# GpSimd's shifted bit pattern as 32-bit additions in five pieces, in a fused attention and gated-MLP kernel

## The chip, the cores and the metric

The kernel runs on one core of a Trainium2 chip. The metric is the device time of one execution in microseconds (us). In this document PE is the matmul engine, PEld its weight loads, ACT the activation engine, DVE the vector engine, POOL (GpSimd) the general-purpose engine, SP the queue that issues transfers. In this kernel PSUM is the memory that the matmuls write to and SBUF the working memory; an eviction copies a result out of PSUM into SBUF. The granted clock is the share of PE's full clock that the profile records as let through.

A time with no other remark is a median of runs. A ratio is the mean time of one kernel's fast runs over that of the other kernel's fast runs of the same rounds, so it isn't quite the ratio of the medians quoted beside it.

## The reference

Layer norm, then attention with 32 heads of size 16 over 2048 positions, plus a gated MLP, plus the input:

```
def reference(A_x, A_wqkv, A_wo, B_x, B_W_gate, B_W_up, B_W_down):
    x = A_x                       # 1 x 2048 x 512, bf16
    xn = _layernorm(x)
    # attention: softmax(q k^T * 16**-0.5) v, 32 heads, then @ wo
    # MLP: h = relu(xn @ W_gate) * (xn @ W_up);  h @ W_down
    return x + _A_ref(xn, A_wqkv, A_wo) + _B_ref(xn, B_W_gate, B_W_up, B_W_down)
```

Some 134 million exponentials are what makes it long: in the kernel before, the 647 instructions of ACT's part of them are busy 742.3 us of a span of 793.6.

## The kernel before

ACT computes most exponentials (647 instructions). For 108 groups of score tiles, DVE computes them instead (16 of these groups with help from GpSimd), by building bf16 bit patterns from an integer. One such group goes like this (cuts marked with `...`):

```
# d1: four evictions out of PSUM, 128x512 each: score -> integer bit pattern tp
e.tensor_scalar(dring[...].bitcast(U16), ps_b[...], 0.25 * LOG2E * 128.0, ..., op0=ALU.mult, op1=ALU.add)
# d2, d3, d5: correction terms from tp, on DVE, SBUF to SBUF
G.op("DVE", 600, ... bitwise_or ...,  lock=True, name="d2")
G.op("DVE", 600, ... bitwise_and ..., lock=True, name="d3")
G.op("DVE", 1140, ... tensor_tensor mult ..., lock=True, name="d5")
# the shifted pattern ts_ = tp + 36: on GpSimd in some groups, on DVE (d4) in the others
if g in on_pool:
    cuts = [2048 * k // N_ADD for k in range(N_ADD + 1)]          # N_ADD = 7
    for a, z in zip(cuts, cuts[1:]):
        o = G.op("POOL", 100 + int(P_NS * (z - a)),                # P_NS = 1.4
                 lambda e, a=a, z=z: e.tensor_scalar(b(ts_, U16)[:, a:z], b(tp, U16)[:, a:z], float(SHIFT), None, op0=ALU.add),
                 reads=[tp], ..., name="pm", lock=True)
else:
    G.op("DVE", 600, ... the same addition on all 2048 ..., name="d4", lock=True)
```

Four quadruples of matmuls per group (PV) then multiply the four patterns with the values; the last reads `ts_`.

Nothing here is dispatched at run time. `G.op(engine, duration, function, ...)` only records an instruction with an **assumed duration**. A planner then places all of them, and each engine gets a fixed list with semaphore waits. For the instructions with `lock=True` the planner keeps GpSimd and DVE apart: a piece on GpSimd is placed beside a DVE instruction without the mark, such as the eviction d1, and only if it is planned to end by about the end of that instruction:

```
if y.lock or at + o.dur > y.start + y.dur + self.SLIP:    # y: DVE's current instruction, SLIP = 100 ns
    continue
```

The softmax here doesn't subtract the row's maximum and nothing guards it: scores larger than these inputs give would overflow.

Of the kernel before, what the change touches and what calls it, by code (L numbers as in the profile page):

```python
# [9 lines left out]
U16 = mybir.dt.uint16  # L10
FP16 = mybir.dt.float16
ACTF = mybir.ActivationFunctionType
ALU = mybir.AluOpType
# [19 lines left out]
NWS = 3  # L33
NQ = 3
NDR = 9
N_ADD = 7
P_NS = 1.4
P_PRIO = -2.4
POOL_AT = ((), (2,), (), (6,), (), (1,), (), (2,), (), (3,), (), (2,), (), (2,), (), (4,), (), (1,), (), (3,), (), (4,), (), (2,), (), (3,), (), (1,), (), (1,), (), (1,))
KD = (1, 5, 9, 13)  # L40
# [36 lines left out]
SHIFT = 36  # L77
# [379 lines left out]
def bass_parallel_sum__mha_block__glu_gated_reglu__prompt_kernel(  # L457
# [16 lines left out]
    with ExitStack() as es:  # L474
        def sb(name, shape, dt):
            return es.enter_context(nc.sbuf_tensor(name, shape, dt))
# [3 lines left out]
        hmask = sb("hmask", [128, 2], FP32)  # L480
        expo = sb("expo", [128, 4], FP32)
        minus = sb("minus", [128, 1], FP32)
        warm = sb("warm", [128, 2], FP32)
        stats = sb("stats", [128, NT, 6], FP32)
        mv = sb("mv", [128, NT, 2], FP32)
# [34 lines left out]
        G = Graph()  # L520
# [23 lines left out]
             reads=[t_pid], writes=[t_pid], prio=-890)  # L544
        G.op("DVE", 100, lambda e: e.tensor_scalar(hmask[:, 1:2], pid[:, 0:1], 1.0 / 16.0, None, op0=ALU.mult),
             reads=[t_pid], writes=[t_mask], prio=-889)
        G.op("DVE", 100, lambda e: e.tensor_scalar(hmask[:, 0:1], pid[:, 0:1], -1.0 / 16.0, 1.0, op0=ALU.mult, op1=ALU.add),
             reads=[t_pid], writes=[t_mask0], prio=-888)
# [2 lines left out]
        G.op("POOL", 300, lambda e: e.affine_select(out=ident[:], in_=ident[:], compare_op=ALU.not_equal, fill=1.0,  # L551
                                                    base=0, pattern=[[-1, 128]], channel_multiplier=1),
             reads=[t_id], writes=[t_id], prio=-898)
        t_vones, t_woz, t_minus = Tile(), Tile(), Tile()
        G.op("POOL", 200, lambda e: e.memset(minus[:], -1.0), writes=[t_minus], prio=10)
        t_qz = [Tile(), Tile()]
        t_qt0 = Tile("qr", P_qr, [0])
        G.op("POOL", 500, lambda e: e.memset(qT[:, 0, :], 0.0), writes=[t_qt0], prio=-600)
# [4 lines left out]
             reads=[t_id32], writes=[t_id32], prio=60)  # L563
# [13 lines left out]
        for i in range(2):  # L577
            dma(lambda e, i=i: e.dma_start(q_scr[i, :, DH:2 * DH, :], qT[:, 0, :]), 128,
                reads=[t_qt0], writes=[t_qz[i]], prio=-600)
# [35 lines left out]
        for j in range(4):  # L615
            for ee in range(2):
                dma(lambda e, j=j, ee=ee: e.dma_start(Wo_p[32 * j:32 * j + DH, ee, :], wo_src[NGG - 1, j, ee, :, :]), 16,
                    reads=[t_woz], writes=[Tile()], prio=40)
# [579 lines left out]
        def score(e, bank, t):  # L1198
            c4, gg, ee, kt, j = t
            return e.matmul(bank, kT[32 * j:32 * j + 32, gg, 128 * kt:128 * kt + 128],  # L1200
                            qm[32 * j:32 * j + 32, t_q[(c4, gg)].slot, ee, :], start=True, stop=True, tile_position=(32 * j, 0))
# [3 lines left out]
        def dve_exp(g, u):  # L1205

            tp, tm, tn, ts_ = (Tile("dr", P_dr) for _ in range(4))
            t4 = [g + (j,) for j in range(4)]
            prev_d, mine = list(last_d), []
            for j, t in enumerate(t4):  # L1210
                ts = Tile("ds", P_b, D_BANKS)
                G.op("PE", 225, lambda e, t=t, ts=ts: score(e, ps_b[:, ts.slot, :], t), mode="row", rows=(j,), reads=[t_q[t[:2]], t_k[(t[1], t[3] // 4)], t_kfirst] + ([t_q1] if t[:3] == (0, 0, 1) else []), writes=[ts],
                     prio=u + D_WAIT, name="dsc", after=u - D_AHEAD, order=prev_d if D_SEQ else ())
                G.ops[-1].acq.append(tp)
                mine.append(G.ops[-1])
                o = G.op("DVE", 610, lambda e, j=j, ts=ts: e.tensor_scalar(dring[:, tp.slot, 512 * j:512 * j + 512].bitcast(U16), ps_b[:, ts.slot, :],  # L1216
                                                                    0.25 * LOG2E * 128.0, 128.0 * (127.0 - LOG2_SUM), op0=ALU.mult, op1=ALU.add),
                         reads=[ts], writes=[tp], prio=u - 960, name="d1")
                for w in tp.w[:-1]:
                    o.deps.pop(w, None)  # L1220
                if tp in o.acq:
                    o.acq.remove(tp)
            last_d[:] = mine

            def b(t, dt=BF16):
                return dring[:, t.slot, :].bitcast(dt) if dt is not BF16 else dring[:, t.slot, :]
            G.op("DVE", 600, lambda e: e.tensor_scalar(b(tm, U16), b(tp, U16), 0xFF80, None, op0=ALU.bitwise_or),  # L1227
                 reads=[tp], writes=[tm], prio=u - 3, name="d2", lock=True)
            G.op("DVE", 600, lambda e: e.tensor_scalar(b(tn, U16), b(tp, U16), 0xFF80, 1, op0=ALU.bitwise_and, op1=ALU.bitwise_or),  # L1229
                 reads=[tp], writes=[tn], prio=u - 2.5, name="d3", lock=True)  # L1230
            G.op("DVE", 1140, lambda e: e.tensor_tensor(b(tm), b(tp), b(tm, I16), ALU.mult), reads=[tm, tp], writes=[tm], prio=u - 3, name="d5", lock=True)  # L1231
            if g in on_pool:
                cuts = [2048 * k // N_ADD for k in range(N_ADD + 1)]
                for a, z in zip(cuts, cuts[1:]):
                    o = G.op("POOL", 100 + int(P_NS * (z - a)), lambda e, a=a, z=z: e.tensor_scalar(b(ts_, U16)[:, a:z], b(tp, U16)[:, a:z], float(SHIFT), None, op0=ALU.add),  # L1235
                             reads=[tp], writes=[ts_] if a == 0 else [], prio=u + P_PRIO, name="pm", lock=True)
                    if a:
                        o.order.add(ts_.w[0])
                        ts_.w.append(o)
            else:  # L1240
                G.op("DVE", 600, lambda e: e.tensor_scalar(b(ts_, U16), b(tp, U16), float(SHIFT), None, op0=ALU.add),  # L1241
                     reads=[tp], writes=[ts_], prio=u - 2.4, name="d4", lock=True)
            for i in range(4):
                where[g + (i,)] = ((tp, tn, tm, ts_), lambda k, i=i: dring[:, (tp, tn, tm, ts_)[k].slot, 512 * i:512 * i + 512])
# [3 lines left out]
        for u, cl in enumerate(units):  # L1248
# [6 lines left out]
            while dve_todo and dve_todo[0][0] <= u:  # L1255
                dve_exp(dve_todo.pop(0)[1], u)
# [30 lines left out]
        for i in range(4):  # L1287
# [26 lines left out]
            if i not in FIN_PE:  # L1314
                G.op("DVE", 610, lambda e, i=i, to_=to_, tz=tz: e.tensor_tensor(xn_sb[:, to_.slot, :], bank_of(tz), resid(i), ALU.add),
                     reads=[tz, t_res[m]], writes=[to_], prio=NU + 10 + i)
            else:
                G.op("ACT", 600, lambda e, to_=to_, tz=tz: e.activation(xn_sb[:, to_.slot, :], bank_of(tz), ACTF.Copy),
                     reads=[tz], writes=[to_], prio=NU + 10 + i)
            dma(lambda e, m=m, to_=to_: e.dma_start(out2[128 * m:128 * (m + 1), :], xn_sb[:, to_.slot, :]), 128, reads=[to_], writes=[Tile()],  # L1320
                prio=NU + 10 + i, stream=("out", m % 8))
# [50 lines left out]
```

## Time and profile before

| | before |
|---|---|
| time, median of 2 runs | 794.23 us (793.71 to 794.74) |
| PE / ACT / DVE / GpSimd busy | 760.1 / 750.7 / 733.8 / 290.8 us |
| GpSimd's pieces of the shifted pattern | 112, median 958 ns, planned 510 |
| mean granted PE clock (profiled run, 795.38 us) | 0.994 |

A busy share says how long an engine had something in hand, not who set the pace: with three engines over 92%, look for what makes a busy engine wait. A wait line reads "who <- for whom: us in total, times, longest". The prediction shows the main lines of this profile. One view that it doesn't show, the busy time per stretch, matters later. The columns of this view of the kernel before are: stretch, its length, busy us and instructions of PE, PEld, DVE, ACT, POOL, then the granted PE clock, DMA share and GB/s.

```profile
383.00:387.00 4.00, 2.66 (x35) 0.70 (x27) 3.42 (x6) 3.56 (x4) 4.00 (x2) 1.00 0.25 66
387.00:391.00 4.00, 3.80 (x31) 0.89 (x35) 2.36 (x4) 1.95 (x2) 0.14 (x1) 0.57 0.29 74
444.00:448.00 4.00, 3.49 (x39) 0.98 (x39) 1.86 (x4) 1.61 (x3) 0.46 (x1) 0.70 0.09 34
677.00:681.00 4.00, 3.68 (x32) 0.92 (x32) 1.98 (x3) 1.41 (x2) 3.07 (x2) 0.59 0.04 7
```

The clock was 1.00 before 387 us and 0.57 in the four us after it. Windows of one microsecond read 0.50 from 388 to 391 us, so this is half clock, and a mean of 0.57 over 4 us means (1 - 0.57) * 2 * 4 = 3.4 us of it. PE looks *busier* in that stretch (3.80 of 4.00 us) while it gets through fewer instructions (31, against 35 in the four us before), and ACT works only 1.95 us. The page shows hardly any of this: its row of the PE clock has a 9 in all 40 slices.

### The profile page before, as it was taken

To read this page: it belongs to the slowest core of one execution; us is meant where nothing else is said; L and a number is where in the kernel's file an instruction comes from. 1 tells how busy PE (TensorE), PEld (TensorE's weight loads), DVE (VectorE), ACT (ScalarE), POOL (GpSimd) and SP (SyncE) were. 2 spreads that over 40 slices of the span, in tenths; PEclk is the share of its full clock that TensorE was granted. 3 is DMA by queue.
4 is the path that set the end of the run, shared out by engine and by line. 5 is a ranking of instruction groups with operands and counts; after the bars stand their busy time and mean duration, and the time that the engine had idled before them with its cause. 6 is when DMAs were issued, how large, how long until landed. Compare 5 with 4: busy or idle time off the path is not lost.

```text
span 793.6 us, 21752 instructions
## 1 busy us (share of the span) xinstructions
PE 760.1 (96%) x9518; PEld 229.3 (29%) x9518; DVE 733.8 (92%) x1132; ACT 750.7 (95%) x662; POOL 290.8 (37%) x284
## 2 busy tenths in 40 slices
PE   8999999899999999999899998999999999999997
PEld 3322222222223222222222232222222222222233
DVE  8699999999999979999889799999899989799985
ACT  6999999999999999999899898999999999899994
POOL 3152242624162261703433426263333523335240
PEclk9999999999999999999999999999999999999999
DMA  7312122212111221222221121232310123221000
GB/s 219 101 45 59 50 55 55 55 35 68 43 45 46 65 58 42 69 69 69 61 56 35 36 76 51 55 80 63 87 42 27 37 69 86 58 75 43 23 28 28
DMA packets 95759, 46.86 MB, mean 59 GB/s; under 512 B 69936, under 2 KB 91824, under 8 KB 95664
## 3 DMA queue, kind: packets, MB, share of 16 engines
q1 hardware_dynamic: 95664, 45.46, 21.1%
q8 instruction: 75, 1.23, 0.6%
q14 instruction: 20, 0.16, 0.1%
HBM read 36.70 MB, written 8.50 MB: 57 GB/s over the span
## 4 chain that ended last, share of the span: by engine, by line
DVE 46%; PE 42%; POOL 6%; ACT 4%; issue 1%; DMA 0%; DVEq 0%
DVE dring L1216 18%; PE ps_b L732 16%; PE ps_b L1176 12%; PE ps_sc L1200 11%; DVE dring L1231 7%; POOL dring L1235 5%; DVE dring L1227 5%; DVE dring L1229 4%; ACT ring L1276 4%; DVE dring L1241 3%; DVE up_sb L940 2%; PE ps_b L1200 2%; DVE hT L944 2%; DVE Wv L1110 1%; POOL rrec L1128 1%
## 5 line engine op out<-in xcount | busy, mean ns | idle before, releaser
L1276 ACT ACTIVATE ring<-ps_sc 128x1536 bf16<-128x1536 f32 (+1 forms) x647 | 742.3, 1260 | 26.0 <-PE ps_b L1200 7.9
L1216 DVE TENSOR_SCALAR dring<-ps_b 128x512 uint16<-128x512 f32 x432 | 289.3, 684 | 32.3 <-PE ps_b L1200 28.4
L1200 PE MATMUL ps_sc<-qm,kT 32*128 32x512 bf16 x1616 | 262.7, 386 | 4.4 <-ACT ring L1276 2.8
L1200 PE MATMUL ps_b<-qm,kT 32*128 32x512 bf16 x432 | 162.0, 386 | 4.7 <-DVE dring L1216 1.5
L1235 POOL TENSOR_SCALAR dring<-dring 128x293 uint16<-128x293 uint16 (+1 forms) x112 | 126.1, 1148 | 86.8 <-DVE dring L1216 22.0
L1176 PE MATMUL ps_b<-ring,v_aug 128*17 128x512 bf16 x1616 | 143.7, 383 | 3.3 <-DVE Wv L1110 2.0
L1138 POOL TENSOR_TENSOR x_sb<-Wv,rb 128x128 bf16<-128x128 f32 x100 | 46.6, 469 | 246.2 <-DVE dring L1231 65.7
L1231 DVE TENSOR_TENSOR dring<-dring 128x2048 bf16<-128x2048 bf16 x108 | 131.5, 1219 | 0.0
L1200 PEld LDWEIGHTS ps_sc<-qm,kT 32*128 32x128 bf16 x1616 | 62.0, 91 | 226.2 <-ACT ring L1276 175.2
L1128 POOL TENSOR_TENSOR rrec<-rsum,minus 128x16 f32<-128x16 f32 x30 | 99.4, 3314 | 76.0 <-DMA rsum<-Wv 76.0
L1176 PE MATMUL ps_b<-dring,vd 128*17 128x512 bf16 x864 | 80.0, 382 | 9.9 <-POOL dring L1235 8.8
L1176 PE MATMUL ps_b<-dring,v_aug 128*17 128x512 bf16 x864 | 79.3, 381 | 1.0 <-DVE dring L1229 0.7
L1227 DVE TENSOR_SCALAR dring<-dring 128x2048 uint16<-128x2048 uint16 x108 | 76.0, 708 | 0.5
L1229 DVE TENSOR_SCALAR dring<-dring 128x2048 uint16<-128x2048 uint16 x108 | 75.5, 702 | 0.3 <-PE ps_b L1176 0.3
L732 PE MATMUL ps_b<-xnT,wus 128*32 128x512 bf16 x896 | 71.4, 390 | 1.3 <-DVE dring L1216 0.5
L732 PE MATMUL ps_b<-xnT,wgs 128*32 128x512 bf16 x896 | 69.2, 386 | 1.0 <-DVE up_sb L940 0.2
L1241 DVE TENSOR_SCALAR dring<-dring 128x2048 uint16<-128x2048 uint16 x92 | 63.8, 699 | 1.1 <-PE ps_b L1176 0.6
L1176 PEld LDWEIGHTS ps_b<-ring,v_aug 128*17 128x17 bf16 x1616 | 36.4, 89 | 63.2 <-issue 41.2
L1200 PEld LDWEIGHTS ps_b<-qm,kT 32*128 32x128 bf16 x432 | 38.5, 91 | 52.5 <-DVE dring L1216 31.0
L732 PE MATMUL ps_b<-Wd,hT 128*32 128x512 bf16 x672 | 49.8, 389 | 0.0
L940 DVE COPY up_sb<-ps_b 128x512 f32<-128x512 f32 x56 | 38.3, 683 | 5.2 <-PE ps_b L732 5.1
L1176 PEld LDWEIGHTS ps_b<-dring,vd 128*17 128x17 bf16 x864 | 20.5, 89 | 45.5 <-POOL dring L1235 11.2
(110 smaller groups left out, 405.5 us busy)
## 6 DMA issues: line engine op xcount, KB each, us to landing
rb<-rec_scr SPq DMA_DIRECT2D x30, 256.0 KB
wus<-in_B_W_up_dram SPq DMA_DIRECT2D x56, 128.0 KB, 2.6
wgs<-in_B_W_gate_dram SPq DMA_DIRECT2D x56, 128.0 KB, 2.3
qm<-q_scr SPq DMA_DIRECT2D x30, 128.0 KB
o_scr<-x_sb SPq DMA_DIRECT2D x25, 128.0 KB
q_scr<-qT SPq DMA_DIRECT2D x17, 128.0 KB
xr_sb<-in_A_x_dram SPq DMA_DIRECT2D x16, 128.0 KB, 2.9
out_dram<-xn_sb SPq DMA_DIRECT2D x16, 128.0 KB, 1.8
```

Source lines behind the costliest of these rows:

```text
L732: ins = e.matmul(bank_of(tile, sub)[32 * j:32 * j + 32, :], st[:, 32 * j:32 * j + 32], mv, start=(i == 0), stop=(i == n - 1), tile_positio ...
L940: G.op("DVE", 610, lambda e: e.tensor_copy(up_sb[:, tup.slot, :], bank_of(tu)), reads=[tu], writes=[tup], prio=slots[1] + EV)
L1128: G.op("POOL", 3000, lambda e: e.tensor_tensor(rrec[:, par, :], rsum[:, par, :], minus[:, 0:1].to_broadcast([128, 16]), ALU.pow), reads=[t ...
L1176: ins = e.matmul(ps_b[32 * j:32 * j + VN, 0, :], v, src[j][1](k), start=(first and k == 0), stop=(last and k == ways - 1), tile_position=( ...
L1200: return e.matmul(bank, kT[32 * j:32 * j + 32, gg, 128 * kt:128 * kt + 128], qm[32 * j:32 * j + 32, t_q[(c4, gg)].slot, ee, :], start=True ...
L1216: o = G.op("DVE", 610, lambda e, j=j, ts=ts: e.tensor_scalar(dring[:, tp.slot, 512 * j:512 * j + 512].bitcast(U16), ps_b[:, ts.slot, :], 0 ...
L1227: G.op("DVE", 600, lambda e: e.tensor_scalar(b(tm, U16), b(tp, U16), 0xFF80, None, op0=ALU.bitwise_or), reads=[tp], writes=[tm], prio=u - ...
L1229: G.op("DVE", 600, lambda e: e.tensor_scalar(b(tn, U16), b(tp, U16), 0xFF80, 1, op0=ALU.bitwise_and, op1=ALU.bitwise_or), reads=[tp], writ ...
L1231: G.op("DVE", 1140, lambda e: e.tensor_tensor(b(tm), b(tp), b(tm, I16), ALU.mult), reads=[tm, tp], writes=[tm], prio=u - 3, name="d5", loc ...
L1235: o = G.op("POOL", 100 + int(P_NS * (z - a)), lambda e, a=a, z=z: e.tensor_scalar(b(ts_, U16)[:, a:z], b(tp, U16)[:, a:z], float(SHIFT), N ...
L1241: G.op("DVE", 600, lambda e: e.tensor_scalar(b(ts_, U16), b(tp, U16), float(SHIFT), None, op0=ALU.add), reads=[tp], writes=[ts_], prio=u - ...
L1276: return e.activation(ring[:, a:a + n, :], ps_sc[:, 3 * k0:3 * k0 + n, :], ACTF.Exp, scale=0.25)
```

## The change

The intent: bit patterns are 16 bits wide, but two of them lie in one 32-bit word. Adding 36 * 65537 to the word adds 36 to both halves, with no carry as long as the lower half doesn't overflow. GpSimd then has 1024 words instead of 2048 elements per group, cut into five pieces instead of seven, and the planner is told a longer time per element.

```diff
-N_ADD = 7
-P_NS = 1.4
+N_ADD = 5
+P_NS = 2.2
...
+        shift2 = sb("shift2", [128, 1], mybir.dt.int32)
...
+        G.op("POOL", 200, lambda e: e.memset(shift2[:], 65537 * SHIFT), writes=[t_shift2], prio=11)
...
-                cuts = [2048 * k // N_ADD for k in range(N_ADD + 1)]
+                cuts = [1024 * k // N_ADD for k in range(N_ADD + 1)]
                 for a, z in zip(cuts, cuts[1:]):
-                    o = G.op("POOL", 100 + int(P_NS * (z - a)), lambda e, a=a, z=z: e.tensor_scalar(b(ts_, U16)[:, a:z], b(tp, U16)[:, a:z], float(SHIFT), None, op0=ALU.add),
-                             reads=[tp], writes=[ts_] if a == 0 else [], prio=u + P_PRIO, name="pm", lock=True)
+                    o = G.op("POOL", 100 + int(P_NS * (z - a)), lambda e, a=a, z=z: e.tensor_tensor(
+                        b(ts_, mybir.dt.int32)[:, a:z], b(tp, mybir.dt.int32)[:, a:z], shift2[:, 0:1].to_broadcast([128, z - a]), ALU.add),
+                         reads=[tp, t_shift2], writes=[ts_] if a == 0 else [], prio=u + P_PRIO, name="pm", lock=True)
```

More of the change, by code (lines that the diff above doesn't have):

```diff
@@ L553, in bass_parallel_sum__mha_block__glu_gated_reglu__prompt_kernel @@
              reads=[t_id], writes=[t_id], prio=-898)
-        t_vones, t_woz, t_minus = Tile(), Tile(), Tile()
+        t_vones, t_woz, t_minus, t_shift2 = Tile(), Tile(), Tile(), Tile()
         G.op("POOL", 200, lambda e: e.memset(minus[:], -1.0), writes=[t_minus], prio=10)
+        G.op("POOL", 200, lambda e: e.memset(shift2[:], 65537 * SHIFT), writes=[t_shift2], prio=11)
         t_qz = [Tile(), Tile()]
```

## The prediction

The 620 ns that it expects of a 32-bit piece was the author's estimate; the trace of the kernel before has no such piece. That the addition on 32-bit words is exact is shown by no run here. By "blocking" it means that DVE's instructions from SBUF to SBUF and GpSimd's pieces take longer when they run at the same time.

> **What bounds the kernel now.** I read the page's busy shares first, then the chain that ended last, then the waits of the matmul engine, then the surroundings of each wait in the timeline. The busy shares and the chain by line (columns: share of the span), from the page of the kernel before:
>
> ```profile
> PE 760.1 (96%) x9518; PEld 229.3 (29%) x9518; DVE 733.8 (92%) x1132; ACT 750.7 (95%) x662; POOL 290.8 (37%) x284
> ...
> DVE 46%; PE 42%; POOL 6%; ACT 4%; issue 1%; DMA 0%; DVEq 0%
> DVE dring L1216 18%; PE ps_b L732 16%; PE ps_b L1176 12%; PE ps_sc L1200 11%; DVE dring L1231 7%; POOL dring L1235 5%; DVE dring L1227 5%; DVE dring L1229 4%; ACT ring L1276 4%; DVE dring L1241 3%; DVE up_sb L940 2%; PE ps_b L1200 2%; DVE hT L944 2%; DVE Wv L1110 1%; POOL rrec L1128 1%
> ```
>
> Three engines are packed: PE 96%, ACT 95%, DVE 92%. GpSimd works 37% of the time, yet the very line that the change edits, L1235, is 5% of the chain, some 40 us. So this idle-looking engine is at times what others wait for. A share of a chain is not a gain: a wait of 2 us at the end of 7 us of GpSimd work puts all 7 us on the chain. The gain has to be read from the waits. The waits of the matmul engine alone (total us, times, longest us):
>
> ```profile
> PE ps_b L1176 <- POOL dring L1235: 8.8, 6, 1.9
> ...
> PE ps_b L1200 <- POOL dring L1235: 1.3, 1, 1.3
> ```
>
> Seven stalls, 8.8 + 1.3 = 10.1 us, of PE's idle time of 793.6 - 760.1 = 33.5 us; no other releaser has more than 2.8. One of the seven, in order of time (start us, length us, instruction, in brackets the idle time before it), from the timeline of 476 to 492 us:
>
> ```profile
> 478.31 1.50 POOL L1235 TENSOR_SCALAR dring<-dring 128x292 uint16<-128x292 uint16 x1 [0.75 <-DVE dring L1229]
> ...
> 480.44 7.34 POOL L1235 TENSOR_SCALAR dring<-dring 128x293 uint16<-128x293 uint16 x6 [0.63 <-DVE dring L1241]
> ...
> 487.83 0.39 PE L1176 MATMUL ps_b<-dring,vd 128*17 128x512 bf16 x4 [1.88 <-POOL dring L1235]
> ...
> 489.46 3.71 ACT L1276 ACTIVATE ring<-ps_sc 128x1536 bf16<-128x1536 f32 x3 [1.86 <-PE ps_b L1200]
> 489.50 0.69 DVE L1216 TENSOR_SCALAR dring<-ps_b 128x512 uint16<-128x512 f32 x1 [1.17 <-PE ps_b L1200]
> ```
>
> The seventh piece ends at 487.78, the matmuls that read the shifted pattern start 0.05 us later after 1.88 us of idleness, and ACT then stands still for 1.86 us and DVE for 1.17 us, because the next scores stood behind those matmuls in PE's fixed order. Such a stall is lost by all three busy engines. I found the others in the same way, at 156.5, 292.6, 387.2, 444.5, 677.3 and 726.0 us (1.59, 1.27, 1.54, 1.48, 1.29, 1.06 us).
>
> Why GpSimd is late: the kernel orders all its instructions in advance with durations it assumes. For one piece of 293 elements it takes 100 + 1.4 * 293 = 510 ns, short enough to lie beside one DVE eviction out of PSUM. Its real length, from the groups by line (minimum/median/maximum ns) and from the page (busy us, mean ns, idle before):
>
> ```profile
> L1235 POOL TENSOR_SCALAR dring<-dring x112: 937/958/2272, 42.6 to 771.3; 128x293 uint16<-128x293 uint16 x64, 128x292 uint16<-128x292 uint16 x48
> ```
>
> ```profile
> L1216 DVE TENSOR_SCALAR dring<-ps_b 128x512 uint16<-128x512 f32 x432 | 289.3, 684 | 32.3 <-PE ps_b L1200 28.4
> L1235 POOL TENSOR_SCALAR dring<-dring 128x293 uint16<-128x293 uint16 (+1 forms) x112 | 126.1, 1148 | 86.8 <-DVE dring L1216 22.0
> ```
>
> 958 ns is nearly twice the assumed 510, and longer than the eviction (684) it should fit beside. So seven pieces slip against the plan by about 7 * 0.45 = 3.1 us in each group.
>
> [...] 958 ns for 293 elements is 3.3 ns each. [...] the trace's own two-input instruction (128x128 bf16 from 128x128, L1138) takes a median of 456 ns[...]. [...] just after pieces that outlast the eviction, L1227 and L1229 take up to 986 and 909 ns in place of 685, and a piece takes up to 2272 in place of 958.
>
> **The change part by part.** The diff leaves the choice of groups alone. The trace has 112 pieces, 112 / 7 = 16 groups (not the 15 of the heading); I expect 16 * 5 = 80.
> 1. GpSimd's own work. [...] A group falls from 7 * 0.958 = 6.7 us to 5 * 0.62 = 3.1 us, and with blocking from 7 * 1.148 = 8.0 to perhaps 3.5. GpSimd's busy time falls by 126.1 - 80 * 0.68 = 72 us, to near 220. That alone is worth nothing, since GpSimd isn't a bound.
> 2. The path that sets the end. The plan now assumes 100 + 2.2 * 205 = 551 ns against the 620 expected: a group slips by 5 * 0.07 = 0.35 us, no longer by 3.1, and needs five evictions to hide beside, not seven. The stalls were 1.1 to 1.9 us; all seven should go or shrink to nearly nothing: PE gets back up to 10.1 us. The ACT gaps straight behind them add up to some 11 to 13 us, so the other engines agree on the size.
> 3. DVE. Its four SBUF-only groups lose (76.0 - 108 * 0.685) + (75.5 - 108 * 0.685) + (63.8 - 92 * 0.684) + (131.5 - 108 * 1.215) = 2.0 + 1.5 + 0.9 + 0.3 = 4.7 us to blocking. A piece of 620 ns ends about when the eviction does, so most of this goes, some 3 us. DVE has slack, so I count 1 us of it.
> 4. The order. Every changed duration makes the planner place other instructions elsewhere on all engines. That has no sign; I give it plus or minus 4 us. Against the gain: with PE at 96% the next limit is near, and stalls removed at one place partly return as waits of PE on ACT or DVE; I take back 2 us.
> One memset of a constant at the start is new, about 0.1 us on an idle GpSimd.
> Sum: 794.2 - 10.1 - 1 + 2 = 785.1; I say 785.5.
>
> **Rivals.** (a) *The stalls turn into others.* If PE's waits on L1235 end and PE, ACT or DVE wait on each other instead, for instance DVE on scores (the wait of L1216 for L1200 is 28.4 us in 37 times), the time stays at 791 to 794. For it: three engines above 92%. Against it: at each stall ACT and DVE stood still too, so none was using the time. (b) *The new instruction is slow.* A broadcast operand or the integer path could take 4 ns a word: a piece near 950 ns as before, still outlasting the eviction. Five pieces are then 4.8 us against 6.7, the slip 5 * 0.4 = 2 us in place of 3.1: about half of the stalls remain, 789 to 791. Nothing in this trace shows 32-bit integers, so I can't exclude it. (c) *More than the sum.* Earlier GpSimd frees the buffers of a group sooner, DVE loses no blocking, and the delayed reciprocals and products behind the pieces (L1128, L1138) come earlier: 778 to 781. For it: DVE is 46% of the chain. Against it: GpSimd is the releaser of only 10 us of PE's idleness. (d) *An unlucky order*, which puts several us of new waits into the plan: 790 to 797.
>
> **Range and chances.** The main path gives 785.5; (b) and (d) pull up, (c) down. Eight in ten: 779 to 792. Faster by over 2% means under 778.3, which needs more than all the waits on GpSimd: 0.09. Slower by over 2% (above 810) needs an engine bound that I see no sign of: 0.01. Within 2%: 0.90.
>
> **What would show it.** Right: 80 pieces of 550 to 700 ns; PE's waits for GpSimd's pieces under 2 us in total; L1235's successor below 2% of the chain; L1227 and L1229 near a mean of 690; PE's share up to about 97%, its busy time unchanged. Step 1 is wrong if a piece is over 800 ns; step 2 is wrong if the waits on GpSimd go and the time doesn't, with PE's idle time still above 30 us under other names; step 4 if waits that weren't there before, on DVE or ACT, carry the difference.

## More of the kernel before

The planner also puts matmuls on zeros ("blanks") into gaps that it foresees on PE. It can't foresee a gap that comes of a wrong duration.

## The result, and the profile after

The changed kernel took 772.16 us (771.55 and 772.78) against 794.23, a ratio of 0.9722 with a 95% interval of 0.9679 to 0.9765: faster by 22 us. The prediction's 785.5 us and its lower end of 779 were both too high.

Lines of the page of the kernel after (instructions moved down by two or three lines in the source; L1218 is the old L1216, L1237 the old L1235, L1202 the old L1200):

```profile
PE 748.2 (97%) x9482; PEld 228.2 (30%) x9482; DVE 725.0 (94%) x1132; ACT 746.0 (97%) x662; POOL 200.3 (26%) x253
...
DVE 48%; PE 42%; ACT 8%; issue 1%; DMA 0%; POOL 0%; DVEq 0%
...
L1218 DVE TENSOR_SCALAR dring<-ps_b 128x512 uint16<-128x512 f32 x432 | 288.0, 683 | 16.7 <-PE ps_b L1202 15.4
...
L1237 POOL TENSOR_TENSOR dring<-dring,shift 128x205 int32<-128x205 int32 (+1 forms) x80 | 42.1, 527 | 108.9 <-DVE dring L1218 37.2
```

There are 80 pieces, as predicted (16 groups; the change was announced for 15). A piece takes 527 ns, close to the 551 planned. GpSimd is gone from the chain (6% before). The waits of PE in the kernel after, largest first:

```profile
PE ps_b L1178 <- DVE Wv L1112: 4.6, 12, 0.9
PE ps_sc L1202 <- ACT ring L1279: 2.8, 6, 0.8
PE ps_b L1202 <- DVE dring L1218: 1.8, 8, 0.4
```

None is for GpSimd, where it was 10.1 us before. So the predicted mechanism is there, and yet the gain is more than twice the predicted 8.7 us. Three further things stand out.

**The clock.** The same three stretches of the kernel after all have a clock of 1.00:

```profile
387.00:391.00 4.00, 4.00 (x60) 1.24 (x56) 2.35 (x4) 4.00 (x4) 0.75 (x2) 1.00 0.26 66
444.00:448.00 4.00, 4.00 (x53) 1.32 (x55) 4.00 (x7) 4.00 (x5) 1.63 (x1) 1.00 0.24 70
677.00:681.00 4.00, 3.94 (x52) 1.25 (x50) 3.99 (x7) 4.00 (x5) 0.00 (x0) 1.00 0.30 72
```

**DVE.** Its SBUF-to-SBUF groups, before and then after (columns: busy us, mean ns, idle before):

```profile
L1231 DVE TENSOR_TENSOR dring<-dring 128x2048 bf16<-128x2048 bf16 x108 | 131.5, 1219 | 0.0
L1227 DVE TENSOR_SCALAR dring<-dring 128x2048 uint16<-128x2048 uint16 x108 | 76.0, 708 | 0.5
...
L1241 DVE TENSOR_SCALAR dring<-dring 128x2048 uint16<-128x2048 uint16 x92 | 63.8, 699 | 1.1 <-PE ps_b L1176 0.6 <-PE ps_b L1200 0.5
```

```profile
L1233 DVE TENSOR_TENSOR dring<-dring 128x2048 bf16<-128x2048 bf16 x108 | 130.9, 1213 | 0.0
L1231 DVE TENSOR_SCALAR dring<-dring 128x2048 uint16<-128x2048 uint16 x108 | 73.7, 685 | 0.0
L1229 DVE TENSOR_SCALAR dring<-dring 128x2048 uint16<-128x2048 uint16 x108 | 73.6, 683 | 0.5
L1244 DVE TENSOR_SCALAR dring<-dring 128x2048 uint16<-128x2048 uint16 x92 | 62.0, 682 | 0.0
```

Before, the four sums (with L1229's 75.5) are 346.8 us, after 340.2: the same instructions take 6.6 us less. The trace of the kernel before shows where. Of the 416 instructions in these groups 33 took over 20 ns more than their group's median, and at the start of 31 of the 33 a piece was running on GpSimd. Of the 112 pieces, 69 took 937 to 961 ns; the other 43 took 1249 ns or more, and each of these overlapped an instruction of these groups by more than 100 ns. This is what blocking stands for here. The evictions out of PSUM (L1216) showed none of it: the longest of 432 took 693 ns, the median is 683.

**ACT.** Its idle time ahead of its exponentials fell from 26.0 us to 6.6.

### The profile page after: what moved, and what is told of

Its sections match the earlier page's. It is cut to its first block, busy times and chain, and to the rows that moved or that the text cites.

```text
span 769.8 us, 21666 instructions
## 1 busy us (share of the span) xinstructions
PE 748.2 (97%) x9482; PEld 228.2 (30%) x9482; DVE 725.0 (94%) x1132; ACT 746.0 (97%) x662; POOL 200.3 (26%) x253
## 4 chain that ended last, share of the span: by engine, by line
DVE 48%; PE 42%; ACT 8%; issue 1%; DMA 0%; POOL 0%; DVEq 0%
DVE dring L1218 19%; PE ps_b L734 16%; PE ps_b L1178 12%; PE ps_sc L1202 11%; DVE dring L1233 8%; ACT ring L1279 7%; DVE dring L1229 5%; DVE dring L1231 4%; DVE dring L1244 3%; DVE up_sb L942 3%; PE ps_b L1202 2%; DVE hT L946 2%; DVE Wv L1112 2%; DVE qT L786 1%; DVE v_aug L828 1%
## 5 line engine op out<-in xcount | busy, mean ns | idle before, releaser
L1218 DVE TENSOR_SCALAR dring<-ps_b 128x512 uint16<-128x512 f32 x432 | 288.0, 683 | 16.7 <-PE ps_b L1202 15.4
L1202 PE MATMUL ps_sc<-qm,kT 32*128 32x512 bf16 x1616 | 260.5, 384 | 4.6 <-ACT ring L1279 2.8
L1202 PE MATMUL ps_b<-qm,kT 32*128 32x512 bf16 x432 | 161.9, 384 | 2.8 <-DVE dring L1218 1.8
L1178 PE MATMUL ps_b<-ring,v_aug 128*17 128x512 bf16 x1616 | 145.4, 381 | 5.7 <-DVE Wv L1112 4.6
L1202 PEld LDWEIGHTS ps_sc<-qm,kT 32*128 32x128 bf16 x1616 | 62.0, 91 | 226.8 <-ACT ring L1279 196.9
L1130 POOL TENSOR_TENSOR rrec<-rsum,minus 128x16 f32<-128x16 f32 x30 | 93.2, 3106 | 110.3 <-DMA rsum<-Wv 110.3
L1229 DVE TENSOR_SCALAR dring<-dring 128x2048 uint16<-128x2048 uint16 x108 | 73.6, 683 | 0.5
L1231 DVE TENSOR_SCALAR dring<-dring 128x2048 uint16<-128x2048 uint16 x108 | 73.7, 685 | 0.0
L1237 POOL TENSOR_TENSOR dring<-dring,shift 128x205 int32<-128x205 int32 (+1 forms) x80 | 42.1, 527 | 108.9 <-DVE dring L1218 37.2
L734 PE MATMUL ps_b<-xnT,wus 128*32 128x512 bf16 x896 | 69.4, 384 | 0.5 <-DVE dring L1218 0.3
L1244 DVE TENSOR_SCALAR dring<-dring 128x2048 uint16<-128x2048 uint16 x92 | 62.0, 682 | 0.0
L1202 PEld LDWEIGHTS ps_b<-qm,kT 32*128 32x128 bf16 x432 | 38.5, 91 | 45.9 <-DVE dring L1218 29.8
L1178 PEld LDWEIGHTS ps_b<-dring,vd 128*17 128x17 bf16 x864 | 20.4, 89 | 33.9 <-issue 12.3
```

What stands on the lines that cost most here:

```text
L734: ins = e.matmul(bank_of(tile, sub)[32 * j:32 * j + 32, :], st[:, 32 * j:32 * j + 32], mv, start=(i == 0), stop=(i == n - 1), tile_positio ...
L1130: G.op("POOL", 3000, lambda e: e.tensor_tensor(rrec[:, par, :], rsum[:, par, :], minus[:, 0:1].to_broadcast([128, 16]), ALU.pow), reads=[t ...
L1178: ins = e.matmul(ps_b[32 * j:32 * j + VN, 0, :], v, src[j][1](k), start=(first and k == 0), stop=(last and k == ways - 1), tile_position=( ...
L1202: return e.matmul(bank, kT[32 * j:32 * j + 32, gg, 128 * kt:128 * kt + 128], qm[32 * j:32 * j + 32, t_q[(c4, gg)].slot, ee, :], start=True ...
L1218: o = G.op("DVE", 610, lambda e, j=j, ts=ts: e.tensor_scalar(dring[:, tp.slot, 512 * j:512 * j + 512].bitcast(U16), ps_b[:, ts.slot, :], 0 ...
L1229: G.op("DVE", 600, lambda e: e.tensor_scalar(b(tm, U16), b(tp, U16), 0xFF80, None, op0=ALU.bitwise_or), reads=[tp], writes=[tm], prio=u - ...
```

## The experiments

Theory A: the pieces were longer than planned, and that cost waits of PE, the half-clock episodes behind them and blocked DVE instructions. Theory B: a large part of the 22 us is the new order that the planner made. Rival C: the blocking of DVE is the main thing. Twelve kernels ran (one of them the change again), in three batches of four, each batch on another chip; the kernel before ran beside each (medians 793.78, 795.05 and 795.01 us). For the runs that keep the kernel before's order, the instruction lists of all engines were compared with those of the kernel before: no difference but the pieces, the blanks where they were added, and the operand where the matmuls read zeros.

### The old order with the new piece

```diff
-  reads=[tp], ... e.tensor_scalar(b(ts_, U16)[:, a:z], b(tp, U16)[:, a:z], float(SHIFT), ...)
+  words = [1024 * k // N_ADD for k in range(N_ADD + 1)]        # still seven, planned 510 ns as before
+  ... e.tensor_tensor(b(ts_, int32)[:, wa:wz], b(tp, int32)[:, wa:wz], shift2 broadcast, ALU.add)
```

> The order of the kernel before on every engine, instruction for instruction (compared, no difference but the form of the pieces), still in seven pieces, but each piece is the 32-bit addition on 146 or 147 words. It separates the speed of the piece from the new order that came with the change. Theory A (lateness: the slow pieces made the matmul engine wait, and those waits also brought three half-clock episodes and knock-on waits): 771 to 777 us, no wait of PE for the pieces, no half clock in the middle, ACT's waits before its exponentials near 7 us instead of 26. Theory B (a large part of the 22 us is the new order's luck): 782 to 787 us, as I predicted for the stalls alone.

775.51 us, ratio 0.9771 (0.9747 to 0.9795). This is theory A: 2.3% of the 2.7% come with the shorter piece in the old order. PE has no wait for a piece left. The pieces now took 426 to 433 ns, and none was blocked (minimum/median/maximum ns):

```profile
L1237 POOL TENSOR_TENSOR dring<-dring,shift x112: 426/429/433, 42.6 to 753.2; 128x146 int32<-128x146 int32 x80, 128x147 int32<-128x147 int32 x32
```

One expectation failed: the profiled run (777.83 us, clock 0.995) has 6.8 us at half clock from 586.9 us on, though PE had waited no longer than 0.2 us in the ten microseconds before. The other three runs have clocks of 0.999 to 1.000.

### The new order with the old piece

```diff
+  lambda e, a=2 * a, z=2 * z: e.tensor_scalar(b(ts_, U16)[:, a:z], b(tp, U16)[:, a:z], float(SHIFT), None, op0=ALU.add)
```

> The order of the changed kernel on every engine, but each of its five pieces is the old 16-bit addition, now on 408 or 410 elements, which should take 410 * 3.2 = 1.3 us against the planned 0.55. Theory A: the plan is missed by 5 * 0.75 = 3.8 us in each group, more than the 3.1 of the kernel before, so 790 to 800 us with waits of PE for the pieces of 10 us or more and several half-clock episodes. Theory B: the new order keeps part of its gain, 778 to 786 us.

796.76 us, ratio 1.0027 (0.9995 to 1.0059). So the new order alone doesn't bring the gain. Whether it helps a little can't be read here, as these pieces are later against their plan, by 5 * (1.446 - 0.551) = 4.5 us per group, than those of the kernel before (3.1). The pieces of this kernel (minimum/median/maximum ns), and PE's wait for them:

```profile
L1237 POOL TENSOR_SCALAR dring<-dring x80: 1237/1446/2428, 43.0 to 772.0; 128x410 uint16<-128x410 uint16 x64, 128x408 uint16<-128x408 uint16 x16
```

```profile
PE ps_b L1178 <- POOL dring L1237: 10.4, 5, 2.6
```

Its runs had granted clocks of 0.994 down to 0.986.

### The matmuls don't wait for the pieces

```diff
- ins = e.matmul(ps_b[...], v, src[j][1](k), ...)
+ ins = e.matmul(ps_b[...], v, zmov if k == 3 and key + (kt,) in on_pool else src[j][1](k), ...)
+ # after planning: these matmuls' waits for GpSimd's pieces are dropped, as they read zeros
```

> The kernel before, order and pieces unchanged, but the 16 quadruples of matmuls that read the shifted pattern from GpSimd read a constant of zeros instead (wrong result on purpose), so that they have nothing to wait for. The slow pieces still block DVE and still hold buffers. Theory A: 8.8 us of PE waits, two of three half-clock episodes (2 * 1.7 us) and some 4 us of knock-on go; 776 to 781 us. Rival C (the blocking of DVE by long pieces, 4.7 us of DVE time, is a main part of the gain): 784 us or more, since that blocking is untouched.

782.68 us, ratio 0.9863 (0.9843 to 0.9883). (Its output is wrong, which doesn't matter for the time. The comparison with the reference still passed, so it is too coarse to notice 16 of these terms; that says how little a pass proves here about the new addition's exactness.) It lies between the 776 to 781 of theory A and the 784 of rival C: the waits and what they bring are worth about 11 us, not 13 to 18, and some 7 us of the long pieces' cost remain.

### Blanks in the wait

```diff
+ # planning done: six blanks ahead of the wait, at the six places where a PV matmul had waited
+ G.before = {pool_pv[i]: [blank_pv] * 6 for i in (2, 5, 7, 8, 9, 14)}
```

> The kernel before, with six quadruples of matmuls on zeros (6 * 0.22 = 1.3 us, adding nothing to the sum) just ahead of the wait, at the six places where PE waited for GpSimd's piece before the matmul that reads it. The stall stays as long as it was, but PE is busy in it. Theory A with the clock as a part: two half-clock episodes of 3.4 us vanish, 2 * 1.7 = 3.4 us and a little knock-on: 788 to 791 us, granted clock 0.998. If the clock is only a bystander: 793 to 797 us.

Its 0.22 us for a quadruple is the distance between two in a row in the trace of the kernel before (starts at 384.40 and 384.62 us).

792.44 us, ratio 0.9984 (0.9962 to 1.0007): by itself inconclusive, and within neither expectation. But every run lists its clock, and that makes it readable. The 23 runs of the kernel before in the three batches lie on a line: 792.3 us at a mean clock of 0.997, 793.8 at 0.995, 795.0 at 0.992 to 0.993, 796.5 at 0.990 to 0.991, 798.18 at 0.989 (correlation -0.97; 0.62 us per 0.001 of clock). The four runs with blanks are 791.18 us at 0.999, 792.35 at 0.998, 792.53 at 0.997 and 793.32 at 0.994, near the same line. In the profiled one the three stretches shown above have a clock of 1.00, and at 387 us the stall itself was as long as before: the waiting matmuls start at 387.14 us, against 387.20. So the time follows the clock. That the blanks raised it is likely, not certain: one of the three stretches follows the wait that got no blanks (still 1.3 us), and its half-clock episode is gone as well. Drawn out to a clock of 1.000, the line gives an estimate of 790.6 us for the kernel before. At its middle clock of 0.993 it pays 4.4 us for half-clock episodes.

### The changed kernel on the chip of the next runs

> The changed kernel unaltered, beside the next runs on one chip, to see what is left between it and the run that had the old order with the new piece (775.4 us in the runs without a half-clock episode). If the new order is worth something of its own: 771 to 773 us. If not: 774 to 776.

771.74 us, ratio 0.9727 (0.9704 to 0.9750). It also shows the clock: two of five runs, at 0.996, took 774.3 us, the others, at 0.999 to 1.000, 771.6 to 771.7. In the profile of one at 0.996, PE was at half clock for 3.4 us from 445.5 us and again from 756.2 us, and no wait of PE over 0.2 us had come in the 15 us before either.

### Only the length of the pieces

```diff
+ # the pieces work on a scratch buffer, each waiting for the one before it
+ e.tensor_scalar(scr_in[:, 0:n], scr_in[:, 0:n], float(SHIFT), None, op0=ALU.add)      # n = 292 or 293
+ # after planning: every wait of other instructions for a piece is dropped
```

> The kernel before in its order, with the old pieces in place and at the same points of GpSimd's queue, but they work on a scratch buffer, one waiting for the other, and nothing in the kernel waits for them or for a buffer of theirs; the matmuls read zeros (wrong result on purpose). What is left of the pieces is only their length on GpSimd[...]. With 782.7 us where only the matmuls' waits were gone and 775.4 with the short piece, this splits the 7.3 us between. Blocking of DVE is the larger part: 779 to 782 us. The late release of buffers (one wait of 1.3 us and what came behind it) is: 776 to 778.

781.30 us, ratio 0.9841 (0.9820 to 0.9862), within the first of its two expectations.

### Pieces of two elements

The same edit with n = 2, each piece on its own two columns, so that none waits for another.

> The same, but each piece is only two elements long, so it neither blocks DVE nor is late: what the old order takes if GpSimd's pieces cost nothing (wrong result on purpose). If the 32-bit pieces are wholly hidden in the old order: within 1 us of 775.4. If they still cost something there: below 773.

775.25 us, ratio 0.9767 (0.9743 to 0.9790). Two things follow. The 6.0 us between this and the run before it are the length of pieces that nobody waits for. And the 32-bit pieces in the old order (775.51) cost nothing that tiny ones don't. DVE's groups show where the 6 us come from; first with the long pieces, then with the tiny ones:

```profile
L1234 DVE TENSOR_TENSOR dring<-dring 128x2048 bf16<-128x2048 bf16 x108 | 131.6, 1220 | 0.0
L1232 DVE TENSOR_SCALAR dring<-dring 128x2048 uint16<-128x2048 uint16 x108 | 76.3, 709 | 0.2 <-PE ps_b L1177 0.2
L1230 DVE TENSOR_SCALAR dring<-dring 128x2048 uint16<-128x2048 uint16 x108 | 75.4, 702 | 0.5
L1245 DVE TENSOR_SCALAR dring<-dring 128x2048 uint16<-128x2048 uint16 x92 | 63.7, 698 | 0.6 <-PE ps_b L1177 0.6
```

```profile
L1234 DVE TENSOR_TENSOR dring<-dring 128x2048 bf16<-128x2048 bf16 x108 | 130.9, 1214 | 0.0
L1232 DVE TENSOR_SCALAR dring<-dring 128x2048 uint16<-128x2048 uint16 x108 | 73.4, 683 | 0.3 <-PE ps_b L1177 0.3
L1230 DVE TENSOR_SCALAR dring<-dring 128x2048 uint16<-128x2048 uint16 x108 | 73.4, 684 | 0.6
L1245 DVE TENSOR_SCALAR dring<-dring 128x2048 uint16<-128x2048 uint16 x92 | 62.2, 681 | 0.6 <-PE ps_b L1177 0.6
```

The sums are 347.0 and 339.9 us. Of 7.1 us of DVE time in which it was blocked, 6.0 reached the end in this order. That GpSimd's own lateness for its other work (the products and reciprocals behind the pieces) has a part in the 6.0 isn't excluded; PE's and ACT's waits in both traces name no such thing.

### The old piece, cut to fit

```diff
-N_ADD = 7
-P_NS = 1.4
+N_ADD = 12
+P_NS = 2.7
```

> The old 16-bit addition with the kernel before's own planner, but cut into 12 pieces of 170 or 171 elements that are planned at 100 + 2.7 * 171 = 560 ns, about what they take (171 * 3.2 = 550 ns). GpSimd's work per group stays near 6.6 us. If what counts is that a piece is as long as planned and fits beside an eviction: 772 to 780 us, without waits of PE for the pieces. If the total work of GpSimd counts: 788 us or more. A new order comes with it, some 4 us either way.

775.55 us, ratio 0.9762 (0.9741 to 0.9783): most of the gain with the old 16-bit instruction, at nearly the old load of GpSimd (284.7 us busy). Its pieces, and who waited for them (the list is empty, the next line follows at once):

```profile
L1235 POOL TENSOR_SCALAR dring<-dring x192: 638/648/1204, 42.6 to 759.7; 128x171 uint16<-128x171 uint16 x128, 128x170 uint16<-128x170 uint16 x64
...
who waited for it (us, times):
busy tenths in 40 slices 0040040304002012300302104030121201203021
```

They took 648 ns, not the 550 I expected (from 937 ns or more for 293 elements in the kernel before, 3.2 ns each) nor the 561 planned: 12 * 0.087 = 1.0 us of slip per group, where the kernel before had 3.1. So the decisive thing isn't how fast GpSimd adds, but that **the pieces don't slip far against their plan**, so that nothing waits for them. They did not stop blocking DVE:

```profile
L1231 DVE TENSOR_TENSOR dring<-dring 128x2048 bf16<-128x2048 bf16 x108 | 130.8, 1212 | 0.1
L1227 DVE TENSOR_SCALAR dring<-dring 128x2048 uint16<-128x2048 uint16 x108 | 75.9, 705 | 1.5 <-PE ps_b L1176 0.8
L1229 DVE TENSOR_SCALAR dring<-dring 128x2048 uint16<-128x2048 uint16 x108 | 74.6, 694 | 1.6 <-PE ps_b L1176 1.6
L1241 DVE TENSOR_SCALAR dring<-dring 128x2048 uint16<-128x2048 uint16 x92 | 63.5, 696 | 1.2 <-PE ps_b L1176 1.2
```

The sum is 344.8 us, 4.9 above that of the tiny pieces, and yet the time is theirs. This run has a new order as well, which may have made up for it, so its exact distance to the others means little.

### Three other orders of the changed kernel

Only the assumed time per word differs: 1.4, 2.0 and 2.4 ns where the change has 2.2.

> The changed kernel, but its planner takes 1.4 ns a word: 387 ns for a piece that took 527. The instructions are the same, only the order differs. The order alone was worth 3.5 us between two plans. If plans differ by chance: 768 to 778 us. A plan that is 140 ns too short slips by 5 * 0.14 = 0.7 us per group, too little for a stall, so nothing beyond chance.

> The same with 2.0 ns a word: 510 ns, closest to the measured 527. If an honest plan is what helps: not slower than the changed kernel's 771.8, thus 768 to 772. If chance rules: anywhere from 768 to 778.

> The same with 2.4 ns a word: 592 ns, 65 ns too long. Pieces then fit beside fewer evictions in the plan, so groups may finish later in it. If chance rules: 768 to 778 us; if a too long plan costs something: 774 or more.

775.21, 775.12 and 773.94 us (ratios 0.9748, 0.9748, 0.9733). The first two have the same list on all engines but PE. Neither the honest nor the long plan stands out, as far as three values can tell. Even the plan of 387 ns for pieces of 527, a slip of 5 * 0.14 = 0.7 us per group, left no wait of PE for a piece. With the change's own 771.7 and the old order's 775.5 the orders lie 3.8 us apart, and the change has the best of those tried.

### More groups on GpSimd

The change with 13 further groups on GpSimd (29 in all) and 2.1 ns a word.

> The changed kernel with 13 further groups given to GpSimd (29 in all), planned at 2.1 ns a word. DVE is relieved of 13 * 0.6 = 8 us and GpSimd gets 13 * 5 * 0.53 = 34 us more. ACT, at 97%, is nearest to a bound, so a gain can only be a few us: 766 to 772 us. If the added pieces come late again somewhere: 774 to 782, with waits of PE for the pieces.

777.09 us, ratio 0.9772 (0.9757 to 0.9786). DVE's busy time fell to 720.6 us, but nothing waited for less: PE has no wait for a piece, and ACT waits 7.4 us in four pieces for PE's PV matmuls, where it was 3.7 in three. So it fell in the range expected for late pieces, but not for that reason; the cause stays open. No version that beats the change was found.

## Why the prediction was wrong

Right were these: seven stalls of PE at the end of late pieces; the count of 80; a piece that fits its plan; and the waits for the pieces gone. The direction and the mechanism held. Two of the signs that it named failed: a piece takes 527 ns, below the 550 to 700, and PE's busy time, said to stay, fell from 760.1 to 748.2 us, where PE busy at half clock is one part. The sum was too small: it stood at 8.7 us, and 22 to 23 were measured. Each part beside its run (medians; for the kernel before 795.0 us, its value at a clock of 0.993):

| part | predicted, us | measured, us | from |
|---|---|---|---|
| half-clock episodes | not counted | 4.4 | clocks of 23 runs, 795.0 to the estimate of 790.6 |
| stalls of PE, direct | 10.1 | 7.9 + 1.4 | 790.6 to 782.7 (matmuls don't wait) to 781.3 (nothing waits) |
| blocked DVE instructions | 1 | 6.0 | 781.3 to 775.3 (tiny pieces) |
| length left in the 32-bit piece | 0 | 0 | 775.3 against 775.5 |
| new order | plus or minus 4 | 3.8 | 775.5 to 771.7 |
| gain given back to the next limit | -2 | not seen | |

**Step 2 failed by what followed a stall.** It took the stalls at their length, and 9.3 us agree with that. But at three of the seven stalls PE's clock was then halved for 3.4 us (worked out above for the one at 387 us). These three followed waits of 1.29 to 1.54 us within otherwise busy stretches. The length of a wait doesn't decide: the stalls of 1.59 and 1.88 us had a clock of 1.00 behind them, and three half-clock episodes in two later profiles (at 586.9 us in the old order with the new piece, at 445.5 and 756.2 us in the changed kernel) came with no wait over 0.2 us in the 10 to 15 us before them. What starts one stays open. Without the stalls they are rarer: all 23 runs of the kernel before have clocks of 0.997 or less, but only one of the four runs with the 32-bit piece in the old order and three of the seven of the changed kernel. The clock of 0.994 stood in the run's record; one question for the stretches behind the stalls would have shown where the missing 0.006 were.

**Step 3 failed in both of its terms.** The blocked time was 6.6 us by the busy sums of the two pages, not 4.7: I subtracted count times median from the busy column. That column counts overlapping records once (76.0 us for 108 of 708 ns, which make 76.5), which loses 1.4 us over the four groups, and the medians of 685 and 1215 lie 1 to 3 ns above the means of the tiny-piece run. And I counted only 1 us of it, "DVE has slack". DVE's 92% was no slack in that order: the tiny-piece run shows 6.0 of 7.1 us reaching the end. The same prediction had quoted DVE's 46% of the chain for rival (c), and that rival, "DVE loses no blocking", pointed the right way and got too little weight; its 778 to 781 us were still too high.

**Step 4** was right in size. I gave it no sign, and it came out at 3.8 us of gain, which is luck: the orders tried with 32-bit pieces span that much, so it is not a property of the new instruction. Taking back 2 us for a next limit was wrong here: ACT, PE and DVE all stood still in the stalls, and after the change their waits shrank together.

Rivals (a), (b) and (d) are ruled out by the waits, by the 527 ns and by the time.

What stays open: the split between the stalls and the clock rests on a fitted line and on four runs with blanks, so 4.4 and 7.9 may each be off by a microsecond or two. Their sum doesn't depend on it: 12.3 us, or 11.1 against the median of that batch, 793.78.

## What to carry to other kernels

In a statically ordered kernel an assumed duration that is far too short is costly: here 448 ns a piece, 3.1 us a group, made PE wait, and 0.7 and 1.0 us a group did not. Find the instructions whose measured length differs from the plan, above all on the engine that looks idle, and cut them to fit the instruction they hide behind, before making them faster. When PE stalls, look at the granted clock of the microseconds after the stall, and count those too. Don't call an engine at over 90% slack: blocked instructions counted nearly in full in one order (6.0 of 7.1 us) and left no trace in the time of another (the 12 pieces), so try it.

## What the traces showed of the hardware

- GpSimd, adding a constant to 16-bit elements: 648 ns for 170 or 171 elements and 958 ns for 292 or 293 (medians), so (958 - 648) / 122 = 2.5 ns per element, an estimate from these two.
- GpSimd, the 32-bit addition of a constant repeated over the row: 429 ns for 146 or 147 words and 527 ns for 204 or 205, so 1.7 ns a word, an estimate from these two. A word holds two 16-bit patterns, so that is 0.8 ns each, a third of the 2.5.
- GpSimd's pieces and DVE's SBUF-to-SBUF instructions blocked each other. In a profile the blocked time isn't shown as a wait, but lies inside the durations: means of 708 and 702 ns in the kernel before for 683 and 685 in the kernel after, and pieces of 1249 to 2272 ns where the others took 937 to 961.
- Half-clock episodes followed PE waits of 1.29, 1.48 and 1.54 us, and others came with no wait over 0.2 us. Of the six told of above, five lasted 3.4 us and one 6.8 us. On the cost, the runs of the kernel before show 0.62 us per 0.001 of mean clock, and the clock goes with nearly all of their spread of 792.3 to 798.2 us (correlation -0.97).
